# One stream of mixed transfers for keys and values in a decode block, with fewer TensorE products

## The chip, the core and the metric

The kernel runs on one core of one Trainium2 chip. Its time is the device time of one execution in microseconds (us). Engines are named as in the profile: PE is TensorE, PEld its weight loads, DVE is VectorE, ACT is ScalarE, POOL is GpSimd, SP issues the DMAs.

## What is computed

One token passes an attention layer and a two-layer perceptron, each with a layernorm whose scale and shift, and whose output's gate, come from a condition vector. All data is float32. The caches dominate: 32 heads x 8192 positions x 192 numbers, once as keys and once as values, 403 MB together.

```python
D, H, Sk, Dh, F = 640, 32, 8192, 192, 1536
mod = (silu(c) @ w_mod).reshape(1, 6, 1, -1)
sa, ca, ga, sb, cb, gb = (mod[:, i] for i in range(6))
h = layernorm(x) * (1 + ca) + sa
q = (h @ wq) split into H heads
scores = einsum("bhqd,bhkd->bhqk", q, k_cache) * Dh ** -0.5
o = einsum("bhqk,bhkd->bhqd", softmax(scores), v_cache)
x = x + ga * (o @ wo)
h = layernorm(x) * (1 + cb) + sb
x = x + gb * (relu(h @ w1 + b1) ** 2 @ w2 + b2)
```

## The kernel before

Every position of a head lies on one of 128 partitions, 64 positions (`NPOS`) to a partition. So a head's keys are a tile of 128 rows of 64 x 192 numbers (49152 bytes a row), its values another of the same size. Both are brought by SP into three slots of 56832 bytes a partition that go round (`slot`, three buffers). `load_k` brings a head's keys; for 30 of 32 heads the row is 7680 bytes longer and carries at its end the weights wq of the next pair of heads or wo of the last one (`WITH_W`), so that it has 56832 bytes. `load_v` brings the values. The keys of the last two heads come in two and four pieces (`CUTS`). The order of all work is the order in which the program writes it; an engine runs its instructions in that order, and a DMA is issued as soon as the slot it writes has been given back by everybody who reads it.

The loop over heads (line 285) does this for each one: issue the loads of keys and values, project the pair before (odd heads), then `keys`: in two halves of 32 positions DVE multiplies the keys in place with the query (line 201), POOL adds the two halves of the last 14 positions' products (line 203), DVE sums the first 18 positions over 192 numbers (line 204) and the last 14 over 96 (line 205). After the first half, `between` computes the next pair's query on PE (`query`, line 181) or adds the last pair's part of the attention output (`attend`, line 267). `softmax` takes the maximum over partitions with a product on PE and a DVE reduction (lines 218 to 222) and the exponentials on ACT (line 228). `values` multiplies them with the values on PE, eight units (`j`) of eight positions (`E`) and three groups of 64 columns each (line 240). `project` divides by the sum, picks the diagonal with a mask and turns the result with another product (lines 254 to 258).

After the loop come the second part: the modulation weights wm1, W1 with the weights of the gate gb, and W2, into the same three slots. `mod` computes six modulation vectors in groups (line 140). The perceptron's first product is at line 343, the gate's in `mod(5, ...)`, a few products that only keep PE busy (line 355), and the last product at line 363, which follows the pieces of W2 as they land.

Of the kernel before, what the change touches and what calls it, by code (L numbers as in the profile page):

```python
# [8 lines left out]
F32 = mybir.dt.float32  # L9
AF = mybir.ActivationFunctionType  # L10
# [21 lines left out]
CUTS = {("k", H - 2): 2, ("k", H - 1): 4}  # L32
WO = 3 * D
WQ = KB * PW
HD = NPOS * DH
SLOT = HD + WO
WITHOUT_W = (1, H - 2)
WITH_W = tuple(h for h in range(H) if h not in WITHOUT_W)
W1_CUT = ((0, 3), (3, 2))
W2_CUT = ((0, 6), (6, 3), (9, 1), (10, 1), (11, 1))  # L40
# [3 lines left out]

@with_exitstack
def block_kernel(ctx: ExitStack, tc: tile.TileContext, kw, ky, vc, wm0, wm1, w1, gb, w2, out):
# [18 lines left out]
    quad = const.tile([P, 32 * NV], F32, name="quad")  # L65
    nc.vector.memset(quad, 0.0)
    for g in range(NV):
        nc.vector.memset(quad[32 * g:32 * (g + 1), 32 * g:32 * (g + 1)], 1.0)
# [31 lines left out]
    def layernorm(x, copies, scale1, shift, name, between=lambda: None):  # L100
# [6 lines left out]
        between()  # L107
# [24 lines left out]
    def mod(first, n, w, steps=(KB,)):  # L132

        ps = psum.tile([P, 512], F32, tag="q", name=f"ps_mod{first}", bufs=2)
        b = 0
        for k in steps:
            for b in range(b, b + k):
                wb = w[:, b].rearrange("p (m n) -> p m n", m=n)
                for g in range(G):
                    nc.tensor.matmul(ps[32 * g:32 * (g + 1), :n * DG], e[:, b:b + 1].to_broadcast([P, 32]),  # L140
                                     wb[:, :, DG * g:DG * (g + 1)], start=(b == 0), stop=(b == KB - 1))
            b += 1
            if b < KB:
                yield
        nc.vector.tensor_copy(mods[:, first:first + n], ps[:, :n * DG].rearrange("p (m n) -> p m n", m=n))  # L145
        yield

    qb_t, k_t, v_t = {}, {}, {}

    def load(src, to, h, what):  # L150
        to[h] = slot(f"{what}{h}")
        n, w = CUTS.get((what, h), 1), src.shape[1]
        for c in range(n):
            a, b = c * HD // n, (c + 1) * HD // n if c + 1 < n else w
            nc.sync.dma_start(to[h][:, a:b], src[:, a:b])

    def load_k(h):

        load(kw[WITH_W.index(h)] if h in WITH_W else ky[WITHOUT_W.index(h)], k_t, h, "k")

    def load_v(h):
        load(vc[h], v_t, h, "v")

    load_k(0)
    next(mod(0, 2, wm0_t[:, :KB * 2 * D].rearrange("p (b n) -> p b n", b=KB)))
# [8 lines left out]
    hR = const.tile([P, KB, P], F32, name="hR")  # L174
    nc.vector.tensor_copy(hR, h1[:, :, None].to_broadcast([P, KB, P]))

    def query(i, w):
        w = w.rearrange("p (b n) -> p b n", b=KB)
        ps = psum.tile([P, 512], F32, tag="q", name=f"ps_q{i}", bufs=2)
        for b in range(KB):  # L180
            nc.tensor.matmul(ps[:, :PW], hR[:, b], w[:, b], start=(b == 0), stop=(b == KB - 1))  # L181
        qb_t[i] = work.tile([P, PW], F32, name=f"qb{i}", tag="qb")
        nc.scalar.activation(qb_t[i], ps[:, :PW], AF.Copy, scale=DH ** -0.5)  # L183
# [3 lines left out]
    att_s = const.tile([P, 2 * DG], F32, name="att_s")  # L187
# [4 lines left out]
    def keys(h, between):  # L192

        q = qb_t[h // 2][:, DH * (h % 2):DH * (h % 2 + 1)]
        sc = work.tile([P, NPOS], F32, tag="sc", name=f"sc{h}")
        t = k_t[h][:, :HD].rearrange("p (i d) -> p i d", d=DH)
        n = NPOS // max(2, CUTS.get(("k", h), 1))
        m = n - POOL * n // 16
        for c in range(NPOS // n):
            pr, s = t[:, c * n:(c + 1) * n], sc[:, c * n:(c + 1) * n]  # L200
            nc.vector.tensor_mul(pr, pr, q[:, None, :].to_broadcast([P, n, DH]))  # L201
            half = pr[:, m:, :DH // 2]
            nc.gpsimd.tensor_add(half, half, pr[:, m:, DH // 2:])  # L203
            nc.vector.tensor_reduce(s[:, :m], pr[:, :m], axis=AX.X, op=ALU.add)  # L204
            nc.vector.tensor_reduce(s[:, m:], half, axis=AX.X, op=ALU.add)  # L205
            between(c)
        return sc
# [8 lines left out]
    def softmax(h, sc):  # L216
        mp = work.tile([P, 1], F32, tag="mp", name=f"mp{h}")
        nc.vector.tensor_reduce(mp, sc, axis=AX.X, op=ALU.max)  # L218
        ps = psum.tile([P, 512], F32, tag="sm", name=f"ps_mx{h}", bufs=2)
        nc.tensor.matmul(ps[:, :P], mp.to_broadcast([P, P]), ident, start=True, stop=True)  # L220
# [3 lines left out]
        p = work.tile([P, NPOS, 32 // E], F32, tag="p", name=f"p{h}", bufs=1)  # L224
# [3 lines left out]
        nc.scalar.activation(p, sc[:, :, None].to_broadcast([P, NPOS, 32 // E]), AF.Exp, bias=nm, accum_out=sp[:, h % 2:h % 2 + 1])  # L228
        if h % 2:
            sum_t[h // 2] = total(sp, f"sum{h // 2}")  # L230
        return p

    def values(h, p):

        t = v_t.pop(h)[:, :HD].rearrange("p (j g n) -> p j g n", g=NV, n=E * ED)
        ps_t[h] = psum.tile([P, 512], F32, tag="o", name=f"ps_o{h}", bufs=3)
        n = NPOS // E
        for j in range(n):
            for g in range(NV):
                nc.tensor.matmul(ps_t[h][32 * g:32 * (g + 1)], p[:, E * j:E * (j + 1)].rearrange("p e r -> p (e r)"),  # L240
                                 t[:, j, g], start=(j == 0), stop=(j == n - 1))
# [3 lines left out]
    def project(i):  # L245
# [3 lines left out]
        inverse(i)  # L249
# [8 lines left out]
        nc.tensor.matmul(os_t[i][:, :n], os_[:n].rearrange("p a d -> p (a d)"), quad[:n], start=True, stop=True)  # L258

    def attend(i, w):  # L260
        oT = work.tile([P, 96], F32, tag="oT", name=f"oT{i}")
        nc.vector.tensor_copy(oT, os_t.pop(i)[:, :96])  # L262
        w = w.rearrange("p (j n) -> p j n", j=3)
# [6 lines left out]
        for j in range(3):  # L270
            for g in range(G):
                nc.tensor.matmul(att_t[0][32 * g:32 * (g + 1), :DG], oT[:, 32 * j:32 * (j + 1)],
                                 w[:, j, DG * g:DG * (g + 1)], start=False, stop=(j == 2))

    def gather():

        nc.scalar.activation(att_s[:64], att_a[:64, :2 * DG], AF.Copy)
        att_t.append(psum.tile([P, 512], F32, tag="o", name="att", bufs=3))
        for g in range(G):
            nc.tensor.matmul(att_t[0][32 * g:32 * (g + 1), :DG], ident[:, 32 * (g // 2):32 * (g // 2) + 1].to_broadcast([P, 32]),  # L280
                             att_s[:, DG * (g % 2):DG * (g % 2 + 1)], start=True, stop=False)
# [3 lines left out]
    for h in range(H):  # L285
        i = h // 2
        if h:
            load_k(h)
        if h == H - 1:
            wm1_t = slot("wm1_t")  # L290
            nc.sync.dma_start(wm1_t[:, :WO + KB * D], wm1[:, :WO + KB * D])
        load_v(h)
        w = k_t[h][:, HD:]

        def between(c):
            if c == 0 and h % 2 and i:
                attend(i - 1, w)
            elif c == 0 and h % 2 == 0 and i + 1 < NPAIR:
                query(i + 1, w)
            elif c == 2 and h == H - 1:  # L300
                gather()

        if h % 2 and i:
            project(i - 1)
        sc = keys(h, between)
        p = softmax(h, sc)
        if h == H - 1:
            next(mod(2, 1, wm1_t[:, WO:WO + KB * D].rearrange("p (b n) -> p b n", b=KB)))
        values(h, p)


    nc.sync.dma_start(wm1_t[:, WO + KB * D:WO + KB * 3 * D], wm1[:, WO + KB * D:])
    w1_t = slot("w1_t")
    for b0, n in W1_CUT:
        nc.sync.dma_start(w1_t[:, b0 * FF:(b0 + n) * FF], w1[:, b0 * FF:(b0 + n) * FF])
    nc.sync.dma_start(w1_t[:, KB * FF:KB * (FF + D)], gb)
    w2_t = slot("w2_t")
    for b0, n in W2_CUT:
        nc.sync.dma_start(w2_t[:, b0 * D:(b0 + n) * D], w2[:, b0 * D:(b0 + n) * D])
# [3 lines left out]

    project(NPAIR - 1)
    attend(NPAIR - 1, wm1_t[:, :WO])
    mod_b = mod(3, 2, wm1_t[:, WO + KB * D:WO + KB * 3 * D].rearrange("p (b n) -> p b n", b=KB), (2, 2, 1))
    next(mod_b)
    x1 = const.tile([P, DG], F32, name="x1")
    nc.vector.tensor_mul(x1, att_t[0][:, :DG], mods[:, 2])
    nc.vector.tensor_add(x1, x1, x_t)  # L330
# [80 lines left out]
```

## Time and profile before

| | |
|---|---|
| time, median of 3 runs | 1057.9 us (1057.46 to 1057.91) |
| span of the profiled execution, first to last instruction | 1055.5 us |
| around the span, against the median | 2.4 us |
| bytes moved | 452.18 MB, 428 GB/s over the span |
| busy: DMA engines (load queue) | 99.3% |
| busy: DVE / PE / POOL / ACT | 79% / 44% / 18% / 3% |

The page gives the busy time of each engine, then the span in 40 slices with a digit for the busy tenths, then the DMA queues with their packets. A group's row names line, engine, operation, what it writes and reads with shapes, the count, and behind the bar the busy time in us, the mean of one in ns, and the idle time before it with what ended it. A row of the chain or the timeline begins with its start and its length in us. The profiled execution's own time is not listed beside the runs; its span is, and the difference of 2.4 us to the median is taken for what lies around it.

### The profile page before, as it was taken

The page shows a single profiled execution, that of the slowest core. Times are in us where ns is not written, and L with a number is a line of the kernel's source. Part 1 is how long each engine was busy: PE and PEld are TensorE (multiplying, and loading weights), DVE is VectorE, ACT ScalarE, POOL GpSimd, SP SyncE. Part 2 cuts the span into 40 slices and gives each one's busy share as a digit, 9 for nine tenths or more (in the row PEclk, how much of TensorE's full clock was granted, in tenths as well). Part 3 has the DMA queues.
Part 4 walks back from the last instruction along what each step waited for, and adds up shares of the span by engine and source line. Part 5 has one row for each costly group of instructions (what it writes and reads, how often), then busy time and mean ns, then how long its engine had stood idle before and what let it go on. Part 6 is the DMA issues. An engine that isn't in the chain of part 4 may idle for free.

```text
span 1055.5 us, 5687 instructions
## 1 busy us (share of the span) xinstructions
PE 463.7 (44%) x2356; PEld 155.0 (15%) x2356; DVE 831.4 (79%) x409; ACT 33.4 (3%) x88; POOL 194.8 (18%) x72
## 2 busy tenths in 40 slices
PE   3234443355543345463334534335453335535446
PEld 1101111111111111120111111101111111111113
DVE  2886878978787987878888687997878798789963
ACT  1000000000000000000000000000000000000000
POOL 0211112211212221212221212221221221122110
PEclk9667666766666766666676666666666666767769
DMA  9999999999999999999999999999999999999997
GB/s 403 435 434 428 432 440 427 441 424 437 433 433 428 440 424 441 424 439 427 431 437 437 422 442 430 428 439 426 439 429 433 428 438 433 434 427 432 424 426 310
DMA packets 11410, 452.18 MB, mean 428 GB/s; under 512 B 1269, under 2 KB 1273, under 8 KB 1785
## 3 DMA queue, kind: packets, MB, share of 16 engines
q1 hardware_dynamic: 11384, 451.83, 99.3%
q8 instruction: 18, 0.29, 0.1%
q14 instruction: 8, 0.06, 0.0%
HBM read 451.82 MB, written 0.00 MB: 428 GB/s over the span
## 4 chain that ended last, share of the span: by engine, by line
DMA 42%; DVE 39%; PE 17%; ACT 1%; issue 1%; SPq 0%; DVEq 0%; ACTq 0%
DMA k<-in_kw 36%; DVE k L201 21%; PE ps_o L240 14%; DVE sc L204 12%; DVE sc L205 5%; DMA k<-in_ky 3%; DMA w_t<-in_w 2%; PE ps_mx L220 1%; DMA wm_t<-in_wm 1%; ACT p L228 1%; PE ps_sum L97 1%; PE ps_mod L140 1%; PE ps_q L181 1%; DVE nm L222 0%; DVE mp L218 0%
## 5 line engine op out<-in xcount | busy, mean ns | idle before, releaser
L201 DVE TENSOR_TENSOR k<-k,qb 128x6144 f32<-128x6144 f32 (+1 forms) x66 | 419.7, 6359 | 141.6 <-DMA k<-in_kw 134.4
L203 POOL TENSOR_TENSOR k<-k 128x1344 f32<-128x1344 f32 (+1 forms) x66 | 194.1, 2941 | 820.9 <-DVE k L201 476.1
L240 PE MATMUL ps_o<-v,p 128*32 128x512 f32 x1536 | 290.4, 731 | 17.2 <-ACT p L228 17.2
L204 DVE TENSOR_REDUCE sc<-k 128x18 f32<-128x3456 f32 (+1 forms) x66 | 240.5, 3644 | 4.3
L220 PE MATMUL ps_mx<-ident,mp 128*128 128x128 f32 x64 | 25.5, 501 | 416.2 <-DVE mp L218 416.2
L240 PEld LDWEIGHTS ps_o<-v,p 128*32 128x32 f32 x1536 | 68.4, 131 | 215.4 <-issue 193.1
L267 PE MATMUL att_a<-k,oT 128*32 128x320 f32 x180 | 49.6, 720 | 114.2 <-DVE oT L262 113.1
L205 DVE TENSOR_REDUCE sc<-k 128x14 f32<-128x1344 f32 (+1 forms) x66 | 99.0, 1500 | 0.0
L220 PEld LDWEIGHTS ps_mx<-ident,mp 128*128 128x128 f32 x64 | 16.1, 312 | 442.8 <-DVE mp L218 421.0
L181 PE MATMUL ps_q<-k,hR 128*128 128x384 f32 x150 | 52.3, 496 | 0.0
L228 ACT ACTIVATE p<-sc,nm 128x256 f32<-128x256 f32 x32 | 16.2, 508 | 760.6 <-DVE nm L222 496.9
L267 PEld LDWEIGHTS att_a<-k,oT 128*32 128x32 f32 x180 | 13.7, 161 | 136.7 <-DVE oT L262 116.7
L222 DVE TENSOR_REDUCE nm<-ps_mx 128x1 f32<-128x128 f32 x32 | 9.3, 291 | 28.5 <-PE ps_mx L220 28.5
L181 PEld LDWEIGHTS ps_q<-k,hR 128*128 128x128 f32 x150 | 27.3, 190 | 27.9 <-issue 11.7
L254 DVE SCALAR_TENSOR_TENSOR om<-ps_o,r,mask 96x512 f32<-96x512 f32 x32 | 23.9, 747 | 6.5 <-PE ps_o L240 5.4
L256 DVE TENSOR_REDUCE os<-om 96x64 f32<-96x512 f32 x32 | 21.8, 682 | 1.1
L140 PE MATMUL ps_mod<-wm_t,silu 128*32 128x320 f32 (+1 forms) x120 | 11.7, 550 | 14.6 <-DVE silu L128 14.6
L97 PE MATMUL ps_sum<-sp,ones 128*128 128x2 f32 x32 | 9.4, 364 | 17.2 <-ACT p L228 17.2
L183 ACT ACTIVATE qb<-ps_q 128x384 f32<-128x384 f32 x16 | 7.9, 491 | 195.2 <-PE ps_q L181 195.2
L97 PEld LDWEIGHTS ps_sum<-sp,ones 128*128 128x128 f32 x32 | 8.0, 312 | 21.9 <-ACT p L228 21.9
L145 DVE COPY mods<-ps_mod 128x320 f32<-128x320 f32 (+1 forms) x4 | 1.6, 398 | 10.2 <-PE ps_mod L140 10.2
L76 DVE COPY small<-wm_t 128x27 f32<-128x27 f32 x1 | 0.2, 179 | 11.2 <-DMA wm_t<-in_wm 11.2
(77 smaller groups left out, 90.9 us busy)
## 6 DMA issues: line engine op xcount, KB each, us to landing
k<-in_kw SPq DMA_DIRECT2D x29, 7104.0 KB, 27.4
v<-in_vc SPq DMA_DIRECT2D x32, 6144.0 KB, 22.1
k<-in_ky SPq DMA_DIRECT2D x1, 6144.0 KB, 28.3
k<-in_ky SPq DMA_DIRECT2D x2, 3072.0 KB, 21.5
k<-in_kw SPq DMA_DIRECT2D x3, 1536.0 KB, 15.5
wm_t<-in_wm SPq DMA_DIRECT2D x1, 4173.5 KB, 12.7
wm_t<-in_wm SPq DMA_DIRECT2D x1, 3200.0 KB, 29.3
wm_t<-in_wm SPq DMA_DIRECT2D x1, 2560.0 KB, 18.2
```

Source lines behind the costliest of these rows:

```text
L97: nc.tensor.matmul(ps[:, :n], ones, src, start=True, stop=True)
L140: nc.tensor.matmul(ps[32 * g:32 * (g + 1), :n * DG], e[:, b:b + 1].to_broadcast([P, 32]), wb[:, :, DG * g:DG * (g + 1)], start=(b == 0), s ...
L181: nc.tensor.matmul(ps[:, :PW], hR[:, b], w[:, b], start=(b == 0), stop=(b == KB - 1))
L201: nc.vector.tensor_mul(pr, pr, q[:, None, :].to_broadcast([P, n, DH]))
L203: nc.gpsimd.tensor_add(half, half, pr[:, m:, DH // 2:])
L204: nc.vector.tensor_reduce(s[:, :m], pr[:, :m], axis=AX.X, op=ALU.add)
L205: nc.vector.tensor_reduce(s[:, m:], half, axis=AX.X, op=ALU.add)
L220: nc.tensor.matmul(ps[:, :P], mp.to_broadcast([P, P]), ident, start=True, stop=True)
L228: nc.scalar.activation(p, sc[:, :, None].to_broadcast([P, NPOS, 32 // E]), AF.Exp, bias=nm, accum_out=sp[:, h % 2:h % 2 + 1])
L240: nc.tensor.matmul(ps_t[h][32 * g:32 * (g + 1)], p[:, E * j:E * (j + 1)].rearrange("p e r -> p (e r)"), t[:, j, g], start=(j == 0), stop=( ...
L254: nc.vector.scalar_tensor_tensor(om[:n], ps_t.pop(h)[:n].rearrange("p (d e) -> p d e", e=E), r2[:n, a:a + 1], mask[:n, None, :].to_broadca ...
L267: nc.tensor.matmul(att_a[32 * g:32 * (g + 1), :2 * DG], oT[:, 32 * j:32 * (j + 1)], w[:, j, 2 * DG * g:2 * DG * (g + 1)], start=(i == 0 an ...
```

## The change

Keys and values no longer come head by head. `plan` cuts the keys of all heads (2048 positions a partition) and the values (256 units of eight positions a partition) into 53 transfers. A full one has 84 x 192 numbers a row (64512 bytes): 44 positions of keys and five units of values; where weights ride along (wo of one pair, or a group of 512 columns of wq) there are fewer positions of keys. A transfer is one slot, so the slots grow from 56832 to 64512 bytes a partition. The plan's 53 transfers have 44 positions of keys in 28 cases, 20 to 42 in the 21 that carry weights, 60 in two, and 64 in the first; the last has only seven units of values. A transfer can end one head and begin the next: the query is applied piece by piece to a head's boundary (`multiply`), scores go into a ring of four heads (`scores`), and the softmax of a head runs when its last position has come. Queries are computed in twelve groups of 512 columns into a ring of three (`query`), without the copy of the normalized input to 128 columns. On each transfer the order is: queries, value products of heads whose softmax is done, multiply, POOL's addition, division and projection of the pair before, sums, attention output, the short sums, softmax, the remaining value products, and the issue of the third transfer after it (`load(n + 3)`), which goes into the same slot.

On PE, the attention output of a pair takes four products for six (three of 512 columns and one of 96 rows by 384), the queries 60 for 80, modulation is computed in one go for vectors 2 to 4 and for the gate in two groups of 320 columns (`gate`), the two turns by a product with a constant matrix become transposes, and the warm-up is two products over all 128 rows for eight over 32. (In the profile each product counts twice.) The last weights come as wm1 in two pieces, W1 with gb in two, and W2 in three; before they were two, three and five.

The diff, cut to its core:

```diff
-CUTS = {("k", H - 2): 2, ("k", H - 1): 4}
-SLOT = HD + WO
+QC = 512
+NQ = H * DH // QC
+UNIT = E * DH
+SLOT = 84 * DH
+VPC = 5
+W1_CUT = (3 * FF, KB * FF + KB * D)
+W2_CUT = (8 * D, 11 * D, 12 * D)
+WM_CUT = (WO + 9 * D, WO + 15 * D)
+def plan():
+    chunks, kp, vp, q, o = [], 0, 0, 1, 0
+    while kp < H * NPOS or vp < H * NPOS // E:
+        room, w = SLOT, []
+        if o < NPAIR - 1 and 2 * (o + 1) * NPOS // E <= vp:
+            w.append(("o", o))
+            o, room = o + 1, room - WO
+        used = (QC * (q - 2) - 1) // DH + 1 if q > 2 else 0
+        if q < NQ and kp >= NPOS * (QC * q // DH) - 3 * NPOS // 2 and kp >= NPOS * used:
+            w.append(("q", q))
+            q, room = q + 1, room - WQ
+        if not chunks:
+            nk, nv = NPOS, 0
+        else:
+            nk = min(H * NPOS - kp, (room - VPC * UNIT) // DH)
+            nv = min(H * NPOS // E - vp, (room - nk * DH) // UNIT)
+            while nv and ((vp + nv - 1) // (NPOS // E) + 1) * NPOS > kp + nk:
+                nv -= 1
+            nk = min(H * NPOS - kp, (room - nv * UNIT) // DH)
+        chunks.append((kp, nk, vp, nv, w))
+        kp, vp = kp + nk, vp + nv
+    return chunks
...
+    def gate(m, w):
+        ps = psum.tile([P, 512], F32, tag="q", name=f"ps_mod{m}", bufs=2)
+        for b in range(KB):
+            for k in range(2):
+                nc.tensor.matmul(ps[64 * k:64 * (k + 1), :2 * DG], e[:, b:b + 1].to_broadcast([P, 64]),
+                                 w[:, b, 2 * DG * k:2 * DG * (k + 1)], start=(b == 0), stop=(b == KB - 1))
+        for g in range(G):
+            r = slice(32 * g, 32 * (g + 1))
+            nc.scalar.activation(mods[r, m], ps[r, DG * (g % 2):DG * (g % 2 + 1)], AF.Copy)
+    def load(n):
+        if n < len(PLAN):
+            chunk_t[n] = slot(f"chunk{n}")
+            m = width(PLAN[n])
+            pieces = [(kv[start[n]:start[n] + P * m].rearrange("(p n) -> p n", p=P), (m,))]
+        else:
+            name, src, cuts = (("wm1_t", wm1, WM_CUT), ("w1_t", w1, W1_CUT), ("w2_t", w2, W2_CUT))[n - len(PLAN)]
+            chunk_t[name] = slot(name)
+            n, pieces = name, [(src, cuts)]
...
+                nc.sync.dma_start(chunk_t[n][:, a:b], src[:, a:b])
...
-            nc.tensor.matmul(ps[:, :PW], hR[:, b], w[:, b], start=(b == 0), stop=(b == KB - 1))
+            nc.tensor.matmul(ps, h1[:, b:b + 1].to_broadcast([P, P]), w[:, b], start=(b == 0), stop=(b == KB - 1))
...
-        nc.tensor.matmul(ps[:, :P], mp.to_broadcast([P, P]), ident, start=True, stop=True)
+        nc.tensor.transpose(ps[:, :P], mp.to_broadcast([P, P]), ident)
...
-            for j in range(3):
-                for g in range(2):
-                    nc.tensor.matmul(att_a[32 * g:32 * (g + 1), :2 * DG], oT[:, 32 * j:32 * (j + 1)],
-                                     w[:, j, 2 * DG * g:2 * DG * (g + 1)], start=(i == 0 and j == 0), stop=(i == NPAIR - 2 and j == 2))
+            for j in range(NV):
+                nc.tensor.matmul(att_a[96:, :512], oT[:, j:j + 1].to_broadcast([P, 32]), w[:, j, :512],
+                                 start=(first and j == 0), stop=(last and j == NV - 1))
+            nc.tensor.matmul(att_a[:96, :NV * (D - 512)], oW.rearrange("p j r -> p (j r)"), w[:, :, 512:],
+                             start=first, stop=last)
...
-    for h in range(H):
+    load(2)
+    for n, (kp, nk, vp, nv, extra) in enumerate(PLAN):
+        t = chunk_t.pop(n)
...
+        for v in range(vp, vp + nv):
+            if v not in late:
+                values(vt[:, v - vp], v)
+        if nk:
+            multiply(kt, kp, nk)
+            m = nk - POOL * nk // 16
+            half = kt[:, m:, :DH // 2]
+            nc.gpsimd.tensor_add(half, half, kt[:, m:, DH // 2:])
...
+            project(project_now)
+        if nk:
+            scores(kt[:, :m], kp)
...
+        if nk:
+            scores(half, kp + m)
+        if done is not None:
+            softmax(done)
...
+        for v in late:
+            values(vt[:, v - vp], v)
...
+        load(n + 3)
...
-    next(mod(5, 1, gb_t))
+    gate(5, gb_t)
...
-        for g in range(G):
-            nc.tensor.matmul(idle[32 * g:32 * (g + 1)], ones[:, :32], w1_t[:, k, :512], start=True, stop=True)
+        nc.tensor.matmul(idle, ones, w1_t[:, k, :512], start=True, stop=True)
```

More of the change, by code (lines that the diff above doesn't have):

```diff
@@ L31, with width, block_kernel @@
 POOL = 7
-CUTS = {("k", H - 2): 2, ("k", H - 1): 4}
 WO = 3 * D
-WQ = KB * PW
-HD = NPOS * DH
-SLOT = HD + WO
[L37 to L40, printed above, removed]
+QC = 512
+NQ = H * DH // QC
+RING = 3 * QC
+SRING = 4 * NPOS
+WQ = KB * QC
+UNIT = E * DH
[4 more added lines that the diff above has]
+WM_CUT = (WO + 9 * D, WO + 15 * D)
 WARM = 2
 EPS = 1e-5
+def plan():
[19 more added lines that the diff above has]
+        kp, vp = kp + nk, vp + nv
+    assert q == NQ and o == NPAIR - 1
+    return chunks
+def width(chunk):
+    return chunk[1] * DH + chunk[3] * UNIT + sum(WO if t == "o" else WQ for t, _ in chunk[4])
+PLAN = plan()
 @with_exitstack
-def block_kernel(ctx: ExitStack, tc: tile.TileContext, kw, ky, vc, wm0, wm1, w1, gb, w2, out):
+def block_kernel(ctx: ExitStack, tc: tile.TileContext, kv, wm0, wm1, w1, w2, out):
     nc = tc.nc
@@ L98, in total, with layernorm @@
         return ps[:, :n]
-    def layernorm(x, copies, scale1, shift, name, between=lambda: None):
+    def layernorm(x, copies, scale1, shift, name):
         n = x.shape[1]
@@ L130, in block_kernel, with mod @@
     mods = const.tile([P, 6, DG], F32, name="mods")
-    def mod(first, n, w, steps=(KB,)):
+    def mod(first, n, w):
         ps = psum.tile([P, 512], F32, tag="q", name=f"ps_mod{first}", bufs=2)
[L135 to L138, printed above, removed]
-                for g in range(G):
[L140 to L144, printed above, removed]
-        nc.vector.tensor_copy(mods[:, first:first + n], ps[:, :n * DG].rearrange("p (m n) -> p m n", m=n))
-        yield
@@ L148, in block_kernel @@
[L148 to L165, printed above, removed]
+        for b in range(KB):
+            wb = w[:, b].rearrange("p (m n) -> p m n", m=n)
+            for g in range(G):
+                nc.tensor.matmul(ps[32 * g:32 * (g + 1), :n * DG], e[:, b:b + 1].to_broadcast([P, 32]),
+                                 wb[:, :, DG * g:DG * (g + 1)], start=(b == 0), stop=(b == KB - 1))
@@ new lines, in block_kernel @@
+    chunk_t = {}
+    start = [sum(width(c) for c in PLAN[:n]) * P for n in range(len(PLAN))]
+    def load(n):
[7 more added lines that the diff above has]
+            n, pieces = name, [(src, cuts)]
+        for src, cuts in pieces:
+            a = 0
+            for b in cuts:
+                nc.sync.dma_start(chunk_t[n][:, a:b], src[:, a:b])
+                a = b
@@ L190, in block_kernel, with multiply, scores @@
     query(0, wm0_t[:, KB * 2 * D:KB * 2 * D + WQ])
[L192 to L207, printed above, removed]
+    sc = const.tile([P, SRING], F32, name="sc")
+    def multiply(t, first, n):
+        a = first
+        while a < first + n:
+            h = a // NPOS
+            b = min(first + n, NPOS * (h + 1))
+            pr = t[:, a - first:b - first]
+            q = qb[:, DH * h % RING:DH * h % RING + DH]
+            nc.vector.tensor_mul(pr, pr, q[:, None, :].to_broadcast([P, b - a, DH]))
+            a = b
+    def scores(src, first):
+        a, n = first, src.shape[1]
+        while a < first + n:
+            b = min(first + n, (a // SRING + 1) * SRING)
+            nc.vector.tensor_reduce(sc[:, a % SRING:a % SRING + b - a], src[:, a - first:b - first], axis=AX.X, op=ALU.add)
+            a = b
     ri_t, ps_t, sum_t = {}, {}, {}
@@ L283, in block_kernel @@
     x_t = spread(x_c, KB, "x_t")
     bbt = spread(bbc, FB + KB, "bbt")
-    for h in range(H):
[L286 to L300, printed above, removed]
-                gather()
[L303 to L309, printed above, removed]
@@ L336, in scale_b @@
         return cb1
-    hT2 = columns(layernorm(x1, 32, scale_b, lambda: mods[:, 3], "ln2", lambda: next(mod_b)), DG, "hT2")
+    hT2 = columns(layernorm(x1, 32, scale_b, lambda: mods[:, 3], "ln2"), DG, "hT2")
     pf = psum.tile([P, 512], F32, tag="q", name="ps_f", bufs=2)
```

147 lines of the change are left out of this document (89 added, 58 removed).

## The prediction

> **What bounds the kernel now.** I read the page first: the span, the engines' totals, the slices of the DMA row and the queues.
>
> ```profile
> span 1055.5 us, 5687 instructions
> PE 463.7 (44%) x2356; PEld 155.0 (15%) x2356; DVE 831.4 (79%) x409; ACT 33.4 (3%) x88; POOL 194.8 (18%) x72
> ...
> DMA  9999999999999999999999999999999999999997
> ...
> DMA packets 11410, 452.18 MB, mean 428 GB/s; under 512 B 1269, under 2 KB 1273, under 8 KB 1785
> ...
> q1 hardware_dynamic: 11384, 451.83, 99.3%
> q8 instruction: 18, 0.29, 0.1%
> ```
>
> The DMA engines are busy from the first slice to the last but one; no compute engine comes near that. 451.83 MB pass in one queue. Its 11384 packets are 79 loads of 128 rows and 16 completion writes each (79 x 144 = 11376) and a few for the output. Next I read busy time by stretch, with the DMA share and the rate as the last two columns and PE's clock before them:
>
> ```profile
> 120.00:900.00 780.00, 343.41 (x1568) 108.91 (x1562) 635.32 (x271) 20.32 (x60) 151.31 (x50) 0.68 1.00 433
> ...
> 952.00:966.00 14.00, 4.37 (x19) 1.89 (x18) 13.04 (x6) 0.60 (x2) 3.03 (x1) 0.62 0.99 423
> 980.00:994.00 14.00, 4.54 (x20) 1.49 (x23) 12.90 (x11) 0.60 (x2) 3.03 (x1) 0.54 1.00 424
> ...
> 1030.00:1040.00 10.00, 5.89 (x81) 3.00 (x82) 5.40 (x16) 0.26 (x1) 0.00 (x0) 1.00 1.00 422
> 1040.00:1045.00 5.00, 5.00 (x56) 2.51 (x52) 0.35 (x1) 0.00 (x0) 0.00 (x0) 0.66 1.00 421
> 1045.00:1048.00 3.00, 3.00 (x62) 1.92 (x56) 2.57 (x7) 0.00 (x0) 0.00 (x0) 1.00 0.84 335
> 1048.00:1050.00 2.00, 1.98 (x60) 1.63 (x55) 0.00 (x0) 0.00 (x0) 0.00 (x0) 1.00 0.56 209
> 1050.00:1055.50 5.50, 1.57 (x36) 0.50 (x27) 0.65 (x2) 0.00 (x0) 0.00 (x0) 0.90 0.03 12
> ```
>
> Three things stand here. For 780 us the share is 1.00 and the rate 433 GB/s, so no wait of an issue leaves the queue dry, and the waits that the chain strings together (keys, DVE, PE, keys) only say who freed a buffer. Where rows are short (24 KB at 952, 12 KB at 980) the share stays near 1.00 and the rate falls to 423 to 424: a row costs something beside its bytes. And from 1045 on engines run out one after another (0.84, 0.56), so the end is set by the last of the 16, not by their mean. Last I read the chain's ends:
>
> ```profile
> 0.74 12.70 DMA wm_t<-in_wm
> ...
> 24.75 6.27 PE ps_q L181 x10
> ...
> 1032.07 19.60 DMA w_t<-in_w
> ...
> 1051.71 0.52 PE ps_y L363 x8
> ```
>
> The last bytes of W2 land at 1051.67; products, two DVE steps and the output take the remaining 3.8 us. The span leaves 2.4 us to the median of the runs shown, 1057.9; I add that to every result.
>
> **Bytes and rows.** The change moves the same bytes: twelve query groups of 512 columns are sixteen of 384, and wo, W1, W2 and the modulation weights keep their size. At 433 GB/s it is the same stream. What falls is the number of loads: wm0 1, the stream 53, wm1 2, W1 with gb 2, W2 3, together 61 where 79 were. That is 18 x 128 / 16 = 144 rows fewer on each engine.
>
> The price of a row comes from the windows. The long stretch has rows of 56832 and 49152 bytes (7104 and 6144 KB over 128), mean 52992; at 433/16 = 27.06 bytes a ns that is 1958 ns. The stretch at 980 has mostly rows of 12288 bytes at 424/16 = 26.5, 464 ns. The difference, 40704 bytes in 1494 ns, gives 27.2 bytes a ns and leaves 12 ns a row. The 24 KB stretch would by the same working give 40 ns; that is one rounded rate over few packets, and nothing excludes zero. So 144 rows bring between 0 and 5.8 us; I take 12 ns, from the row in which the fixed part weighs most: **-1.8 us**.
>
> ```profile
> k<-in_kw SPq DMA_DIRECT2D x29, 7104.0 KB, 27.4
> v<-in_vc SPq DMA_DIRECT2D x32, 6144.0 KB, 22.1
> ```
>
> The Trainium skill (DMA: Bandwidth & Descriptors, "Anatomy of one DMA — SWDGE (gpsimd) path") gives a fixed cost of about 2.0 us for each DMA, measured on the path that GpSimd issues; by that the 18 loads would bring an estimated 36 us. The share of 1.00 over 780 us disagrees: a 7104 KB load takes 16.8 us of the stream at 433 GB/s and lands 27.4 us after its issue, so its start lies under the load ahead of it.
>
> **Does the queue stay full?** One full transfer is 64512 x 128 bytes = 8.26 MB, 19.1 us at 433 GB/s. Three slots mean that the slot of a transfer must be given back within 38.2 us of its landing. DVE's prices:
>
> ```profile
> L201 DVE TENSOR_TENSOR k<-k,qb 128x6144 f32<-128x6144 f32 x62 | 406.3, 6553 | 141.6 <-DMA k<-in_kw 134.4 <-ACT qb L183 4.4 <-DMA k<-in_ky 2.8
> ...
> L204 DVE TENSOR_REDUCE sc<-k 128x18 f32<-128x3456 f32 x62 | 232.7, 3753 | 4.1
> ...
> L205 DVE TENSOR_REDUCE sc<-k 128x14 f32<-128x1344 f32 x62 | 95.7, 1543 | 0.0
> ...
> L254 DVE SCALAR_TENSOR_TENSOR om<-ps_o,r,mask 96x512 f32<-96x512 f32 x32 | 23.9, 747 | 6.5 <-PE ps_o L240 5.4
> L256 DVE TENSOR_REDUCE os<-om 96x64 f32<-96x512 f32 x32 | 21.8, 682 | 1.1
> ...
> L222 DVE TENSOR_REDUCE nm<-ps_mx 128x1 f32<-128x128 f32 x32 | 9.3, 291 | 28.5 <-PE ps_mx L220 28.5
> ...
> L218 DVE TENSOR_REDUCE mp<-sc 128x1 f32<-128x64 f32 x32 | 7.0, 220 | 1.1
> ```
>
> For 44 positions: multiply 44/32 x 6.55 = 9.0, 25 full sums 25/18 x 3.75 = 5.2, 19 half sums 19/14 x 1.54 = 2.1, together 16.3 us. A head that ends adds 0.22 + 0.9 (wait for PE) + 0.29 = 1.4, a pair 2 x (0.75 + 0.68) and small steps, 3.2. With 44/64 of a head per transfer that is 16.3 + 1.0 + 1.1 = 18.4 of 19.1 us: DVE keeps up, barely, in a run of full transfers, and gains time in those with weights (20 to 34 positions). The two transfers with 60 positions (numbers 15 and 38) cost 12.3 + 7.1 + 2.9 + 1.4 + 3.2 = 27 us, 8 more than they last; the two full ones behind start late and catch up only at the next one with weights. Even there the slot comes free some 27 us after landing, the last value products included, 11 us ahead of the 38.2. That is cover about as now (27.4 - 16.8 = 10.6 us for keys). At the start query 0 grows from 6.27 by a third, wm0 with 128 more columns of wq a block is 0.33 MB, 0.76 us, longer and the copy before it (hR) goes; the first slot is free near 33 us, and the first three loads, 19.1 MB, last until 44. Edits hidden by this cover cost nothing: the scores' ring, the split multiplies, ACT's copies, the projection between multiply and sums. If the cover went, each us of late issue would be one us of the end.
>
> **TensorE's products.** By the diff the products in PE's count fall: attention output 12 to 8 a pair (-60), queries 160 to 120, modulation 160 to 100, warm-up 16 to 4; the two transposes may take one pass for two (up to -48). PE is not the bound, so its busy time pays nothing. But its code comes by DMA: 18 fetches of 16 KB for 2 x 2356 instructions, 262 to a fetch. 172 to 220 products fewer are 344 to 440 instructions, 1.3 to 1.7 fetches. The DMA view of the last 55 us, then of the last 25, shows what they cost:
>
> ```profile
> q8 instruction: 3, 0.05, 0.4%
> ...
> q8 instruction: 2, 0.03, 0.5%
> ```
>
> 0.5% of 16 x 25.5 us is 2.0 us for two: one fetch holds one engine for 1 us. As the last engine sets the end, a late fetch that goes is worth 0 (another engine's) to 1.0 us (its own): **-0.5 us**.
>
> **The tail.** The order of the last loads stays, but W1's last two blocks now share a load with gb. The rest of the chain behind it:
>
> ```profile
> 1033.44 1.26 PE L140 MATMUL ps_mod<-wm_t,silu 128*32 128x320 f32 x16
> 1033.69 0.33 DVE L329 TENSOR_TENSOR x<-att,mods 128x160 f32<-128x160 f32 x1 [1.15 <-PE att L272]
> ...
> 1039.02 0.34 DVE L82 STREAM_TRANSPOSE hT<-ln_h 128x160 f32<-128x160 f32 x1
> ...
> 1039.47 5.13 PE L343 MATMUL ps_f<-w_t,hT 128*32 128x384 f32 x40 [2.10 <-issue]
> ...
> 1044.38 1.57 PE L140 MATMUL ps_mod<-w_t,silu 128*32 128x160 f32 x40
> ...
> 1045.74 1.93 PE L355 MATMUL ps_warm<-w_t,ones 128*32 128x512 f32 x16
> ...
> 1047.46 3.16 PE L363 MATMUL ps_y<-w_t,fT 128*32 128x160 f32 x80
> ```
>
> W2 is 3.93 MB, 9.1 us at 433 GB/s, W1 with gb 5.57 MB, 12.9. Call the landing of the last byte E: W1's last piece lands at E - 9.1, the modulation weights at E - 22.0. Their last 16 products, now 480 columns wide (1.5 x 1.26 = 1.9 us), x1 and the layernorm (1033.69 to 1039.36, 5.7 us) give hT2 near E - 14, before W1's last piece. Behind that piece 16 of the 40 products of f remain (2.1 us at the row's mean), gate takes 320 columns in two groups where four took 160 (2 x 1.57 = 3.1), the warm-up 1.9, eleven blocks of y 88/80 x 3.16 = 3.5: E - 9.1 + 10.6 = E + 1.5 before the last block, where now these are just done at E. The other end: f at the clock 1.00 instead of 0.66 (1.4), gate and warm-up by the distance of the rows' starts (2 x 1.36 = 2.7 and 1.7), y at the pace of the stretch at 1048 (60 products in 1.98 us: 2.9): 8.7 us, E - 0.4, which costs nothing. So 0 to +1.5 us; the clock was 1.00 on both sides of the 0.66, which is nearer the second end, and I take **+0.4 us**.
>
> Sum: -1.8 - 0.5 + 0.4 = -1.9 us on 1055.5, a span of 1053.6 and a time of **1056.0 us**.
>
> **Rivals.**
> - *The engines end together* (chance 0.12). Idle shares at the end are 0.16 x 3 + 0.44 x 2 + 0.97 x 1.7 = 3.0 us of each engine. If fewer fetches halve or remove that, the change is -1.8 - 1.5 to -1.8 - 3.0: 1053.1 to 1054.6. For it: the skew is there. Against: only one or two of 18 fetches go.
> - *Each load leaves a gap in the stream* (0.02), and 18 gaps go. A share of 1.00 is 0.995 or more; that leaves 3.9 us over some 50 loads in the 780 us, 0.08 us each, 1.4 us for 18: on top of the forecast, 1054.6. The skill's rule above would make it an estimated 1022. Against both: rate and share already hold all the bytes.
> - *The tail eats it* (0.12). If the clock is halved while PE waits for W1's last piece, f, gate, warm-up and y take twice 8.7 us: E + 8.3, and with the 2.3 won 1063.9; if it recovers after gate, E + 3.7, 1059.3. It decides from 2.3 us of loss on. For it: the clock fell to 0.66 at just this place. Against: PE's waits there are short.
> - *Longer rows stream slower* (0.10, slower than before). 432 of 452 MB come in rows of up to 64512 bytes, and eight of them lie 504 KB apart in memory where now 444 and 384 KB do. Each 0.4% of rate is 4.2 us; from 0.2% on the gain is gone; 1% gives 1066. Against: 48 and 56 KB rows share one rate. The Trainium skill (the same page, "Latency and other measured facts") reports 207 against 214 GB/s where rows of a copy lie 512 KiB apart; by its ratio, an estimate, the kernel would lose 3%, 34 us; no row here has such a distance.
> - *Nothing changes* (0.02): the row cost is zero and tail and fetches cancel, 1057.9.
>
> **How the numbers follow.** The forecast's own case has 0.62. With a row at 12 ns the bounds of fetches and tail (-1.0 to 0, 0 to +1.5) give -2.8 to -0.3, 1055.1 to 1057.6; with a row at nothing the upper end is +1.5, 1059.4. 0.2% is 2.1 us, about what a measurement can tell from no change; the forecast lies at that line, so I split it 0.30 faster, 0.32 same. Faster: 0.30 + 0.12 + 0.02 = 0.44. The tail case is half same, half slower: same 0.32 + 0.06 + 0.02 = 0.40, slower 0.06 + 0.10 = 0.16. The range 1053.6 to 1059.4 reaches from inside the first rival, which a row of 24 ns would give too, to that upper end, which holds the milder tail case; it leaves out the rate, the halved clock and the far end of the first rival.
>
> **What would show it.** Right: 61 x 144 packets and a few in the load queue, DMA share 1.00 at 433 GB/s in the middle, 16 or 17 code fetches, last W2 landing near 1049.4, 3.8 us behind it. Wrong: a share under 0.99 in the middle (a slot given back late), a rate under 432 at share 1.00 (rows), y's products ending over 1 us after W2's last landing (tail).

## The result and the profile after

The changed kernel takes 1061.82 us (median of four runs, 1060.26 to 1064.02) against 1057.82 before: 1.0040 of its time, 95% interval 1.0026 to 1.0054. It is slower by 4.0 us where 1.9 less were forecast. The profiled run is the fastest of the four, 1060.26 with a span of 1058.5. The times scatter over 3.8 us, where those of before lie within 0.5. Between time and span lie 1.8 us here, and 1.7 to 2.1 in every run that lists both, not the 2.4 added in the forecast: the profile of before was not taken in its median run.

The page of the changed kernel, its rows on span, engines, DMA slices and queues:

```profile
span 1058.5 us, 5158 instructions
...
PE 489.4 (46%) x2136; PEld 137.5 (13%) x2136; DVE 825.6 (78%) x398; ACT 39.1 (4%) x106; POOL 188.4 (18%) x58
...
q1 hardware_dynamic: 8792, 451.83, 98.8%
q8 instruction: 17, 0.28, 0.1%
```

The stream is what the diff says: 8792 packets are 61 loads of 144 and the output's 8, with the bytes of before. PE has 220 products fewer, and yet is busy 26 us longer. By the page's groups the attention output took 49.6 us before and takes 61.8 + 13.4 now, the queries 52.3 and 63.6; the columns that pass are the same in number, in fewer and wider products. Which of this comes from the width is not taken apart here. Busy time by stretch, with the clock that PE was granted (1.00 is full speed), the DMA share and GB/s as the last columns:

```profile
120.00:900.00 780.00, 374.23 (x1467) 100.73 (x1467) 632.51 (x286) 25.19 (x75) 144.80 (x41) 0.71 1.00 433
...
1020.00:1030.00 10.00, 8.09 (x53) 2.44 (x53) 2.45 (x5) 2.03 (x4) 0.00 (x0) 1.00 0.95 393
...
1045.00:1048.00 3.00, 3.00 (x34) 1.13 (x28) 0.94 (x3) 0.00 (x0) 0.00 (x0) 1.00 0.84 339
1048.00:1050.00 2.00, 2.00 (x15) 0.99 (x12) 1.12 (x2) 0.19 (x1) 0.00 (x0) 1.00 0.11 44
```

The middle is unchanged, share 1.00 at 433 GB/s. The loads are done by 1050 (share 0.11 in the last two us, where before it was 0.56), so they end earlier than before. But from 1042.14 on PE is busy without a gap until y is done. The chain of the changed kernel from the attention output ahead of the last softmax on (start, length, what):

```profile
1013.40 4.46 PE att_a L317 x6
...
1018.71 0.59 ACT att_s L329
...
1020.20 0.46 PE att L335 x2
1020.66 0.27 PE ps_mx L264
...
1022.39 7.03 PE ps_o L285 x48
...
1031.61 1.02 PE att L324 x24
1032.63 4.07 PE ps_mod L171 x40
1036.73 0.67 DVE mods L173
1037.42 0.34 DVE x L403
...
1042.14 4.78 PE ps_f L416 x40
1046.92 2.84 PE ps_mod L180 x20
1049.76 1.91 PE ps_warm L427 x4
1051.67 3.44 PE ps_y L435 x96
```

Before, the last piece of this chain was a landing of W2 with eight products behind it. Here no load stands in it: y's 96 products begin at 1051.67, when all of W2 is there. Two rows of the timeline show where the chain loses time first, the last head's maximum on DVE and the step that then waits for PE; a third row, from the kernel before, has the same wait:

```profile
1014.74 0.22 DVE L262 TENSOR_REDUCE mp<-sc 128x1 f32<-128x64 f32 x1
...
1021.02 0.29 DVE L266 TENSOR_REDUCE nm<-ps_mx 128x1 f32<-128x128 f32 x1 [6.07 <-PE ps_mx L264]
```

```profile
1018.49 0.29 DVE L222 TENSOR_REDUCE nm<-ps_mx 128x1 f32<-128x128 f32 x1 [0.89 <-PE ps_mx L220]
```

The maximum is ready at 1014.96. Its transpose stands on PE behind `attend` and `gather` of the pair before, which wait for ACT's copies besides; DVE waits 6.07 us where this wait was 0.89 before.

So the theory for the experiments is: the stream brought what was forecast, and a tail on PE that no longer hides under W2's loads ate that and more. Its parts are the products behind the last attention output (4.07 us, and 0.67 for the copy), the gate (2.84) and the place of `attend`. The kernel before had half of its 80 products of vectors 2 to 4 (as the profile counts) ahead of the last values, in its chain as well:

```profile
1020.12 2.82 PE ps_mod L140 x40
```

The rival: the stream of longer transfers itself costs.

### The profile page after: what moved, and what is told of

Its sections match the earlier page's. It is cut to its first block, busy times and chain, and to the rows that moved or that the text cites. A ratio compares the mean times of both kernels' runs of the same rounds, so it can differ in the third digit from the quotient of the medians.

```text
span 1058.5 us, 5158 instructions
## 1 busy us (share of the span) xinstructions
PE 489.4 (46%) x2136; PEld 137.5 (13%) x2136; DVE 825.6 (78%) x398; ACT 39.1 (4%) x106; POOL 188.4 (18%) x58
## 3 DMA queue, kind: packets, MB, share of 16 engines
q1 hardware_dynamic: 8792, 451.83, 98.8%
## 4 chain that ended last, share of the span: by engine, by line
DMA 55%; DVE 32%; PE 11%; ACT 1%; issue 0%; DVEq 0%; SPq 0%; ACTq 0%
DMA chunk<-in_kv 54%; DVE chunk L241 17%; DVE sc L249 13%; PE ps_o L285 5%; PE att_a L317 2%; DMA wm_t<-in_wm 1%; PE ps_mod L171 1%; PE ps_q L221 1%; DVE om L298 1%; DVE os L300 1%; ACT p L272 1%; PE ps_mx L264 0%; PE ps_f L416 0%; PE ps_sum L131 0%; DVE nm L266 0%
## 5 line engine op out<-in xcount | busy, mean ns | idle before, releaser
L241 DVE TENSOR_TENSOR chunk<-chunk,qb 128x6528 f32<-128x6528 f32 (+15 forms) x82 | 419.8, 5150 | 140.5 <-DMA chunk<-in_kv 135.0
L249 DVE TENSOR_REDUCE sc<-chunk 128x19 f32<-128x1824 f32 (+16 forms) x111 | 334.2, 3043 | 0.4
L365 POOL TENSOR_TENSOR chunk<-chunk 128x1824 f32<-128x1824 f32 (+7 forms) x52 | 187.7, 3609 | 820.9 <-DVE chunk L241 581.5
L285 PE MATMUL ps_o<-chunk,p 128*32 128x512 f32 x1536 | 293.4, 729 | 55.9 <-DMA chunk<-in_kv 40.7
L264 PE MATMUL ps_mx<-ident,mp 128*128 128x128 f32 x32 | 14.0, 438 | 323.8 <-DVE mp L262 323.8
L285 PEld LDWEIGHTS ps_o<-chunk,p 128*32 128x32 f32 x1536 | 66.3, 129 | 253.1 <-issue 177.6
L221 PE MATMUL ps_q<-chunk,ln_h 128*128 128x512 f32 x110 | 63.6, 736 | 40.9 <-DMA chunk<-in_kv 40.9
L317 PE MATMUL att_a<-chunk,oT 128*32 128x512 f32 x90 | 61.8, 843 | 44.4 <-DVE oT L306 44.4
L221 PEld LDWEIGHTS ps_q<-chunk,ln_h 128*128 128x128 f32 x110 | 25.4, 241 | 78.8 <-DMA chunk<-in_kv 45.4
L319 PE MATMUL att_a<-chunk,oW 128*96 128x384 f32 x30 | 13.4, 530 | 0.0
```

What stands on the lines that cost most here:

```text
L221: nc.tensor.matmul(ps, h1[:, b:b + 1].to_broadcast([P, P]), w[:, b], start=(b == 0), stop=(b == KB - 1))
L249: nc.vector.tensor_reduce(sc[:, a % SRING:a % SRING + b - a], src[:, a - first:b - first], axis=AX.X, op=ALU.add)
L264: nc.tensor.transpose(ps[:, :P], mp.to_broadcast([P, P]), ident)
L317: nc.tensor.matmul(att_a[96:, :512], oT[:, j:j + 1].to_broadcast([P, 32]), w[:, j, :512], start=(first and j == 0), stop=(last and j == NV ...
L319: nc.tensor.matmul(att_a[:96, :NV * (D - 512)], oW.rearrange("p j r -> p (j r)"), w[:, :, 512:], start=first, stop=last)
L365: nc.gpsimd.tensor_add(half, half, kt[:, m:, DH // 2:])
```

## The experiments

**1. The gate in four groups again.**

```diff
-    gate(5, gb_t)
+    mod(5, 1, gb_t)
```

> One part undone: the gate's 20 products in two groups of 320 columns go back to 40 in four groups of 160. Theory (the tail on PE ends last: y's products run from 1051.67, 2 us after W2 has landed): the gate takes 1.5 us less and nothing hides that, so 1061.8 becomes 1060.3. Rival (the transfers end last, longer rows stream slower): no change, 1061.8.

1060.47 us (nine runs, 1059.29 to 1066.54; 1.0034 of before, 1.0022 to 1.0046). Its chain:

```profile
1042.34 6.00 PE ps_f L416 x40
1048.34 1.36 PE ps_mod L171 x40
```

40 products in four groups take 1.36 us, the 20 in two groups took 2.84. These rows show the 1.5 us. The medians differ by 1.35, but with runs that scatter over 7 us that is not clear of noise. In this run f took 6.00 for 4.78, which hides the gain in the span.

**2. The modulation taken apart again.** Vector 2 runs while DVE projects the last pair, vectors 3 and 4 in the waits of the layernorm. Before the change vector 2 stood ahead of the last values; its place here is a third one. The diff, shortened:

```diff
-WM_CUT = (WO + 9 * D, WO + 15 * D)
+WM_CUT = (WO + KB * D, WO + 3 * KB * D)
-    project(NPAIR - 1)
+    project(NPAIR - 1, lambda: next(mod(2, 1, wm1_t[:, WO:WO + KB * D]...)))
-    mod(2, 3, wm1_t[:, WO:WO + KB * 3 * D]...)
+    mod_b = mod(3, 2, wm1_t[:, WO + KB * D:WO + KB * 3 * D]..., (2, 2, 1))
+    next(mod_b)    # and two more inside layernorm
```

> One part undone: vector 2 of the modulation is computed while DVE projects the last pair, vectors 3 and 4 in the waits of the layernorm, as before the change (three products' pieces, wm1 cut behind vector 2). Theory: of the 4.1 us of products and 0.7 us of copy that now stand between the last attention product and x1, about 1 us remains in the layernorm, so 3.8 us less, 1058.0. Rival (transfers): 1061.8.

1056.97 us (twelve runs, 1055.53 to 1061.54; 1.0004 of before, 0.9990 to 1.0018), 4.85 less. This is the largest part, and clear of noise; but the median falls between two groups of runs, so its size is not firm. The chain of its profile (a run of 1057.92):

```profile
1032.64 1.07 PE att L332 x24
...
1033.73 0.34 DVE x L412
...
1035.20 1.21 PE ps_mod L174 x16
...
1039.45 5.04 PE ps_f L426 x40
```

x1 follows the attention output at once, and f begins 2.7 us earlier although this chain's attention output comes 1.0 us later: 3.7 us, close to the 3.8 expected. Six runs lie at 1055.5 to 1056.0, five at 1060.4 to 1061.5: more in experiment 7.

**3. Attend early.** For the last but one pair, turn and attend stand right behind the projection, gather behind the last softmax. The diff, shortened:

```diff
             project(project_now)
+        early = wo_t is not None and wo_t[0] == NPAIR - 2
+        if early:
+            turn(project_now)
+            attend(*wo_t)
...
         for v in late:
             values(vt[:, v - vp], v)
+        if early:
+            gather()
```

> Only an order: for the last but one pair, turn and attend stand right behind the projection, ahead of the long sums, and the gathering of the attention output behind the last softmax. Theory: the last head's maximum, ready at 1014.96, waits on PE until 1020.59 behind attend and gather; without that the whole tail starts up to 5 us earlier and ends at the transfers' bound or just above it, 1056.5 to 1057.5. Rival (transfers): 1061.8. If the queue was short of W1 because of the late slot, the last landing moves earlier as well, below 1049.6.

1058.24 us (eleven runs, 1056.97 to 1062.28; 1.0012 of before, 1.0002 to 1.0022), 3.6 less, and above the 1056.5 to 1057.5 expected. Its chain:

```profile
1017.74 0.38 PE ps_sum L131 x2
...
1028.66 4.07 PE ps_mod L171 x40
...
1038.18 6.26 PE ps_f L420 x40
...
1049.20 3.44 PE ps_y L439 x96
```

The modulation starts 4.0 us earlier, y only 2.5: f, now reached at 1038.18, takes 6.26 us. PE's clock in the window, the third number from the end, was 0.61:

```profile
1040.00:1045.00 5.00, 5.00 (x38) 1.54 (x32) 0.48 (x1) 0.00 (x0) 0.00 (x0) 0.61 0.95 398
```

So the order is worth 4 of the "up to 5" us at the start of the tail, and part of that is lost in f. W1's loads are issued at 1019.16 for 1023.43, and the share from 1020 to 1030 is above 1.00 for 0.95.

**4. All three edits.**

> All three together. Theory: 3.8 + 1.5 + 5 us are more than the tail stands over the last landing, so W2's landing bounds again: landing near 1050, 3.8 us of span behind it and 2.4 around, 1056.0 to 1056.5, faster than the kernel before by 1.3 to 1.8 us. Rival (transfers): 1061.8, or at best 1060 if both count.

1055.79 us (eleven runs, 1055.52 to 1056.96), 0.9983 of the kernel before (0.9975 to 0.9992). This is the version that beats both. The chain of its profile:

```profile
1019.74 20.79 DMA w_t<-in_w
...
1040.57 1.52 PE ps_f L430 x16
1042.10 2.67 PE ps_mod L174 x40
1044.76 2.21 PE ps_warm L441 x4
1046.97 3.44 PE ps_y L449 x96
```

A load stands in the chain again: f waits for W1's second piece, landing at 1040.53, and the 16 products, gate, warm-up and y behind it end at 1050.41, near W2's last bytes. The gate, in four groups again, takes 2.67 us here for 1.36 in experiment 1; PE had waited 2.67 us for that piece, and its clock from 1040 to 1045 was 0.69. With the tail back under the loads, the kernel gains 1.9 us on the 1057.71 of the kernel before in the same session. The rival falls.

**5. The first two edits without the third.**

> The first two edits together, attend and gather left where the change put them: is the order needed once the tail's products are back? Theory (each edit counts until W2's landing bounds): 1061.8 - 3.8 - 1.5 stands 0.5 us above the bound, so 1055.8 to 1056.5, with more scatter than the kernel of all three, which has its tail ready 5 us earlier. Rival (attend and gather are the main part): 1058 or more.

1055.80 us (twelve runs), 0.9992 of before (0.9982 to 1.0002). Nine of the runs lie at 1055.5 to 1056.5, three at 1058.8 to 1060.2; with the third edit none of eleven is above 1057. The order is not needed for the median. That it gives the cushion which takes the scatter fits, but three runs of twelve against none of eleven do not show it.

**6. The tail alone, on the kernel before.** Its own stream of loads, but the modulation in one go and the gate in two groups.

> The other side: the kernel before with its own stream of loads, and of the change only the tail's modulation (vectors 2 to 4 in one go behind the last attention product) and the gate in two groups. Theory (tail): 3.8 + 1.4 us more work in the chain, of which 1 to 1.5 us are hidden by W2's landing, so 1061 to 1062, with single runs scattered over some us, as the changed kernel has it. Rival (the stream is what costs): 1057.8 to 1058.5.

1062.04 us (five runs, 1061.04 to 1064.47), 1.0044 of before (1.0032 to 1.0056). Two edits of the tail, with the old stream, make the old kernel as slow as the changed one, and as scattered. This is the most direct measure of what the two cost: 4.2 us. The chain of its profile, which is the run of 1064.47:

```profile
1035.44 4.82 PE ps_mod L140 x40
...
1045.66 5.79 PE ps_f L350 x40
```

**7. Where the scatter comes from.** First three idle products over wm1 in the waits of the last layernorm, so that PE does not pause there.

> PE's clock in the tail: the changed kernel with three idle products over wm1 in the waits of the last layernorm, whose result nobody reads. Theory (the clock falls while PE waits there, and f's first products take 640 ns a step for 320): 1.5 us less in the profile, a median of 1058.5 to 1060.3 and less scatter. Rival (the scatter has nothing to do with the clock): 1061.8 or above, by what the idle products take.

1060.94 us (nine runs, 1058.73 to 1065.82; 1.0033 of before, 1.0020 to 1.0046). The profile shows what was meant:

```profile
1040.66 1.82 PE ps_awake L411 x4
1042.50 3.43 PE ps_f L424 x40
```

f takes 3.43 us for 4.78, with a clock of 1.00 from 1040 to 1045 for 0.66, but the median lies above the 1058.5 to 1060.3 expected, falls by 0.9 only, which is not clear of noise, and the scatter is as wide as before: the pause in the layernorm is not its whole cause. Then the kernel of experiment 2 three times more, each with a profile.

> The kernel of the second experiment once more, for its scatter: its 12 times lay near 1055.7 (six) or 1060.8 (five), one at 1057.9. Theory (PE's clock): where the time is near 1061 the profile shows f, gate, warm-up and y after the layernorm at half rate (640 ns for 320 in f, 533 for 267 in the gate) and the last landing unmoved; where it is near 1055.7, at full rate. Rival (the loads): the last landings of W1 and W2 are some 5 us later in the slow one.

> As e9_scatter_a, a second look at the same kernel: clock (PE's steps at half rate, landings unmoved) against loads (landings 5 us later) where the time is near 1061.

> As e9_scatter_a, a third look at the same kernel: clock (PE's steps at half rate, landings unmoved) against loads (landings 5 us later) where the time is near 1061.

1055.84, 1058.04 and 1057.11 us. Rows of the first, then of the second, from their chains and windows:

```profile
1014.69 3.08 PE att_a L325 x5
...
1023.72 17.25 DMA w_t<-in_w
...
1041.01 1.50 PE ps_f L426 x16
1042.51 2.84 PE ps_mod L187 x20
1045.35 1.91 PE ps_warm L437 x4
1047.26 3.44 PE ps_y L445 x96
```

```profile
1014.70 4.27 PE att_a L325 x5
...
1039.63 5.08 PE ps_f L426 x40
...
1040.00:1045.00 5.00, 5.00 (x44) 1.58 (x38) 0.22 (x1) 0.00 (x0) 0.00 (x0) 0.70 1.01 429
```

The same five products of `attend` take 3.08 or 4.27 us, with the clock from 1015 to 1020 at 0.86 or 0.59, and in the slower run f, reached at 1039.63, goes through a stretch with the clock at 0.70; in the faster one that stretch had 1.00 and f was ahead, waiting for W1. The third run lies between: 3.84 us for the five products, 0.81 in the stretch of f. So the clock goes with the 2.2 us between the first two. No profile of a run near 1061 was caught, so the upper group's 5 us stay open. Each run's mean clock is on record: in experiment 2 it is 0.708 to 0.718 in the five runs near 1061 and 0.717 to 0.726 in the six near 1055.7, but in experiment 3 the slow runs show no lower one.

**8. The price of a row.** The kernel before with every load of keys and values in two halves: 62 loads, 496 rows an engine more.

```diff
-        n, w = CUTS.get((what, h), 1), src.shape[1]
+        n, w = CUTS.get((what, h), 2), src.shape[1]
```

> The price of a row: the kernel before with the loads of keys and values in two halves each, 62 loads and 496 rows on each engine more, all bytes the same. Theory (12 ns a row): 5.9 us more, 1063.7. Rival (a row costs nothing, its short rows' lower rate came from elsewhere): 1057.8. Rival (each load leaves a gap of its own, 2 us): 1180.

1062.24 us (five runs, 1062.05 to 1063.01), 1.0045 of before (1.0033 to 1.0057): 4.4 us for 62 loads, 0.07 each, or 9.0 ns for each of 496 rows. Each load also brings a completion write to every engine; the run cannot tell its price from the rows'. A queue and a window of it:

```profile
q1 hardware_dynamic: 20312, 451.83, 99.4%
```

```profile
120.00:900.00 780.00, 367.63 (x1537) 121.87 (x1540) 630.71 (x273) 20.91 (x62) 151.26 (x50) 0.68 1.00 431
```

The share stays at 1.00 and the rate falls to 431: the price is paid inside the stream, and no gap that the share could show opens between loads.

**9. The price of PE's code.** The kernel of experiment 4 with 16 products of two columns behind the maximum of each of 30 heads.

```diff
+        for _ in range(16 if h < 30 else 0):
+            nc.tensor.matmul(ps[:32, 256:258], ones[:, :32], ident[:, :2], start=True, stop=True)
```

> The price of PE's code: the kernel of all three edits to the tail, with 16 products of two columns more behind each head's maximum (30 heads), 1920 instructions, seven fetches more, 24 for 17. Nobody reads their result. Theory (a fetch holds one engine for 1 us and the last engine sets the end; eight engines take them in turn): about one more for each of the eight, so the last landing 0.7 to 1.0 us later, 1056.6. Rival (fetches are free): 1055.8. Rival (they add up): 7 us, 1062.8.

1057.56 us (eleven runs, 1056.91 to 1058.49), 1.8 more than the 1055.79 of the same kernel without them. That is about twice what was expected. Its code queue, and the last us of its loads:

```profile
q8 instruction: 25, 0.41, 0.2%
```

```profile
1048.00:1049.00 1.00, 0.69 (x21) 0.72 (x25) 0.00 (x0) 0.00 (x0) 0.00 (x0) 1.00 0.51 210
1049.00:1050.00 1.00, 1.00 (x40) 1.00 (x34) 0.00 (x0) 0.00 (x0) 0.00 (x0) 1.00 0.41 161
1050.00:1051.00 1.00, 1.00 (x38) 0.81 (x32) 0.00 (x0) 0.00 (x0) 0.00 (x0) 1.00 0.07 26
```

Eight fetches more put the end of the loads 1 to 1.5 us later (share 0.41 in 1049 to 1050, where experiment 4 has 0.03). They don't add up to 8 us, and they are not free. The share is 0.50, 0.49 and 0.51 in the three us from 1046 on, which is what it would be with half of the 16 engines done and the other half still loading. That eight engines take the fetches in turn fits this, but the view doesn't name the engines, so it is not shown.

## Why the prediction was wrong

**Bytes and rows: right, a little large.** Forecast 12 ns a row, measured 9.0 with the load's own share in it; 18 loads of eight rows are 1.3 us for 1.8. The middle stands at 433 GB/s and share 1.00 with rows of 64512 bytes, so the rival of longer, slower rows is out. The 3% worked out from the Trainium skill (DMA: Bandwidth & Descriptors, "Latency and other measured facts") does not appear; the Trainium skill gives it for a distance of 512 KiB from one partition's row to the next, and here that is 63 KiB, with 504 KiB between rows eight apart. The fixed 2 us a DMA that the Trainium skill gives (DMA: Bandwidth & Descriptors, "Anatomy of one DMA — SWDGE (gpsimd) path"), measured there on another path, do not appear in a full queue: 62 loads more cost 4.4 us, 0.07 each.

**The queue: right in the middle, too good at the end.** The share of 1.00 from 120 to 900 says that no slot came back late there. But W1's slot is given back only behind the last softmax and the first value products of its head: its loads are issued at 1023.43 (1017.41 before), and the share falls to 0.95 from 1020 to 1030 (0.99 before). That is about half a us, and the loads still end earlier than before. The rival of engines that end together is out too: in experiment 4 they still run out one after another (shares of 0.61, 0.53 and 0.31 in the three us from 1046), and its time is not at or below 1054.6.

**Code: right in kind.** 17 fetches for 18, and the transposes take one pass for two. Experiment 9 gives 1.8 us for eight more, 0.2 each on average; the -0.5 for one fetch less was not tested by itself. Rows and code together were forecast at -2.3, and experiments 4 and 5 measured 1.9 and 2.0 below the kernel before.

**The tail: the step that failed.** It was given 0 to +1.5 us and +0.4 in the sum. Against the 1055.8 of the kernels whose tail is hidden it cost 6.0 (1061.8). The failing sentence is that the modulation weights land at E - 22 and only "their last 16 products", x1 and the layernorm stand behind, with hT2, the input of f, near E - 14. I started the tail at a landing. In the trace of after it starts at the last value product (1029.42, with the loads done by 1050 about E - 20.6), because the products stand in program order behind the last attention product, which needs that head. All 40 and their copy, 4.74 us, then lie on the path, and hT2 comes at 1042.1, E - 8. Before, 40 of the 80 products were done ahead of the last values, for 2.82 us in the chain, and the others lay in the layernorm's waits; both stood in the trace I had read. So the change does not put all 4.74 us on top of the old path. Experiment 6 measures what it costs on the kernel before, with the gate: 4.2 us. Experiment 2 gains 4.85 by the median and 3.7 by its chain, with vector 2 in a better place than it had before.

The second omission is PE's order around the last softmax. The new place of `attend` got no term ("Edits hidden by this cover cost nothing" thinks of slots alone); the instruction queued behind it was the transpose for the last head's maximum, and everything after waits for that: 3.6 us by experiment 3. The three undone parts sum by their medians to 1.35 + 4.85 + 3.6 = 9.8, more than the 6.0 that there was to gain, since W2 and W1 bound again below; the first of them is not clear of noise.

The gate was sized rightly (3.1 forecast, 2.84 found), yet "the other end", which cost nothing, assumed that it starts when W1's last piece lands. Where the tail is early enough this is so: in the first of the three further runs of experiment 7, which has the changed kernel's gate, f waits for W1's second piece, and behind it follow 1.5, 2.8, 1.9 and 3.4 us for the 1.4, 2.7, 1.7 and 2.9 worked out. The forecast fits kernels with a covered tail, not the changed one: its span of 1053.6 is 1053.8 in experiment 4. That its time of 1056.0 meets 1055.8 as well is in part luck, as 2.4 us were added for 1.8.

The rival "the tail eats it" named the right place and 1059.3 to 1063.9, but by the clock, with 0.12. The main part was work in line, which experiments 2, 3 and 6 show; that the clock adds the scatter is seen in one pair of runs, 2.2 us apart, and the rest is open.

## What to carry to other kernels

When loads bound the end, the compute behind them has a slack, and a change must be charged for every piece of tail work that it moves onto the path from the last input needed: trace that path back through each in-order queue to the last operand that comes, not to the landing of the weights. Fewer, wider products can be more time on PE: count the columns that pass and the groups that pass side by side. Give the tail some us more cushion than one profile says, since single runs of the same kernel lay 4 to 7 us apart once PE and not a load ended last, and 1.4 us where a load stood in the chain (experiment 4).

## What the runs showed of the hardware

A further load of 128 rows costs 0.07 us in a full queue beside its bytes, 9 ns for each of an engine's rows (experiment 8, rows of 24 to 32 KB for 48 to 56), and rows of 64512 bytes stream at the same 433 GB/s as those of 49152 and 56832. Fetches of PE's code are felt by the loads: eight more made a kernel 1.8 us longer (experiment 9). The same 40 products of f took 3.43 us with the granted clock at 1.00 (experiment 7), 6.26 with 0.61 (experiment 3) and 5.79 where it began at 0.50 (experiment 6). The same gate took 1.36 us in 40 products of 160 columns in four groups, and 2.84 in 20 of 320 columns in two.
